# The first tile's statistics and output ahead of the pooled transposes' copies, and the fifth tile's matmuls beside the other output tiles

## The chip, the cores and the metric

One core of one Trainium2 chip runs the whole program. The metric is the device time of one execution in microseconds (us). Several executions of the changed kernel and of the kernel before are taken in turn on the same chip, and a separate profiled execution gives the trace. The engines are named as the profile names them: PE is TensorE's matmuls, PEld its weight loads, DVE is VectorE, ACT is ScalarE, POOL is GpSimd, SP issues DMAs. A line of a timeline gives start and length in us, engine, line of kernel.py, operation, tile written<-tiles read, shapes and count, and in brackets the engine's idle time before it with what ended it.

## The reference, cut to what matters

A linear attention with 32 memory slots feeds a two-layer network with a layer norm, over 8 batches of 576 rows and 512 columns.

```python
k_m = einsum('bhsm,bhsd->bhmd', a, k); v_m = einsum('bhsm,bhsd->bhmd', a, v)  # pooling, a = softmax(phi)
attn = softmax(scale * q @ k_m^T)                                             # scores
x = (attn @ v_m), heads side by side                                          # 8 x 576 x 512
xn = (x - mean(x)) / sqrt(var(x) + 1e-6) * g_ln
out = x + relu(xn @ w_ch1) @ w_ch2                                            # 512 -> 2048 -> 512
```

The kernel folds v_m and g_ln into w_ch1, so the first layer is computed from the attention weights, and it applies 1/sqrt(var) only at the end. That is why the statistics of x can come late: only the output needs them.

## The kernel before

A loop step handles batch b's layers and, between their matmuls, prepares batch b+1. The second layer (mm2) of a tile of 128 rows is 16 matmuls into `ch_ps`, cut into two halves of eight. The output of a tile adds x and frees its `ch_ps` buffer.

```python
def big(...): psum.tile(..., tag="big", bufs=3)    # kv_ps, o_ps, kvT_ps, sc_ps, w1b_ps, den_ps, h_ps
def one(...): psum.tile(..., tag="one", bufs=2)    # ch_ps

def x_tiles(pr, ts, stats=True):   # o_ps matmuls, then ACT copies o_ps to x_sb           (L420, L426)
def x_stats(pr, t):                # DVE: mean and variance of one tile                  (L439, L440)
def x_rstd(pr, ts):                # ACT: rstd = exp(-0.5 ln(var + eps)), two instructions (L445, L446)
def mm2_out(pr, t):                # DVE: x = ch_ps * rstd + x, then two output DMAs     (L483)
def a_kv(b):                       # PE pooling into kv_ps; DVE copies k, v, reciprocal  (L222, L227, L232)
def a_tr(b):                       # PE transposes k, v; DVE copies kvT, gain, row sums  (L261, L263, L267)
def a_sc(b):                       # PE scores from kvT; ACT exponentials E_sb           (L308, L313)
# ... a_den (L339), a_w1b (L369, L373), a_vb, mm1 (h_ps, L390)

for b in range(1, B):
    odd = b % 2; t = [4, 5, 6, 7, 8] if odd else [0, 1, 2, 3]
    mm1(b, ...)                    # ... 64 matmuls
    half(0);  a_kv(nb);  x_tiles(pr, t[0:2], False);  x_tiles(pr, t[2:4], False);  load(nb + 1)
    half(1);  a_tr(nb);  x_stats(pr, t[0]);  x_stats(pr, t[1]);  a_qT(nb + 1, 0)
    half(2);  a_sc(nb);  x_rstd(pr, t[0:2]);  a_w1b(nb, 0);  mm2_out(pr, t[0])
    half(3);  a_den(nb, finish=False);  mm2_out(pr, t[1]);  x_stats(pr, t[2])   # ...
    half(4);  a_den2(nb)           # half(4) is the third tile: it needs the first tile's ch_ps buffer
    if odd: x_tiles(pr, t[4:5], False)      # the fifth tile; else a_w1b(nb, 1..3)
    # ... half(5) to half(9)
```

Conditions on the first and last steps are cut above. In what follows, step one is b = 1 and step seven, the last, is b = 7. Steps one, three, five and seven are odd and have five tiles.

The softmax here doesn't subtract the row's maximum and nothing guards it: scores larger than these inputs give would overflow.

## Time and profile before

| | before |
|---|---|
| time, median of 3 runs | 253.18 us |
| start-up, to the first mm1 of the loop | 54.7 us |
| steps one to six | 30.05, 25.74, 29.64, 25.74, 29.64, 25.73 us |
| step seven, to the matmuls of its last tile (L471) | 22.89 us |
| the rest | 7.3 us |

The parts are those of the profiled execution, whose span on the core is 251.4 us (its time is 253.22). The step lengths are the distances between successive groups of h_ps matmuls in the chain of waits, which follows the work that ended last back through what released it, and has this form (start, length, what):

```profile
110.47 7.96 PE h_ps L390 x64
...
140.11 7.96 PE h_ps L390 x64
...
165.85 7.96 PE h_ps L390 x64
```

Step three is 140.11 − 110.47 = 29.64 us, step four 25.74 us.

### The profile page before, as it was taken

To read this page: it belongs to the slowest core of one execution; us is meant where nothing else is said; L and a number is where in the kernel's file an instruction comes from. 1 tells how busy PE (TensorE), PEld (TensorE's weight loads), DVE (VectorE), ACT (ScalarE), POOL (GpSimd) and SP (SyncE) were. 2 spreads that over 40 slices of the span, in tenths; PEclk is the share of its full clock that TensorE was granted. 3 is DMA by queue.
4 is the path that set the end of the run, shared out by engine and by line. 5 is a ranking of instruction groups with operands and counts; after the bars stand their busy time and mean duration, and the time that the engine had idled before them with its cause. 6 is when DMAs were issued, how large, how long until landed. Compare 5 with 4: busy or idle time off the path is not lost.

```text
span 251.4 us, 5829 instructions
## 1 busy us (share of the span) xinstructions
PE 236.0 (94%) x2446; PEld 131.6 (52%) x2477; DVE 155.1 (62%) x300; ACT 130.1 (52%) x219; POOL 60.0 (24%) x99
## 2 busy tenths in 40 slices
PE   7878999899999999999999999999999999999993
PEld 2443555447534665367534674467444764476453
DVE  3236773595397655787479646885679537873641
ACT  3154662677364464837382646655581755465220
POOL 8643231027204502090206302270205010000000
PEclk9999999999999999999999999999999999999999
DMA  7999999999996798739973998539892300303133
GB/s 148 192 206 207 206 257 215 282 212 128 211 193 128 130 256 182 146 53 202 249 147 89 142 252 136 123 43 223 200 188 44 78 8 0 86 16 71 44 81 83
DMA packets 41922, 36.82 MB, mean 146 GB/s; under 512 B 17444, under 2 KB 37160, under 8 KB 41896
## 3 DMA queue, kind: packets, MB, share of 16 engines
q0 software_dynamic: 17248, 19.53, 45.8%
q1 hardware_dynamic: 24488, 16.79, 29.2%
q8 instruction: 19, 0.31, 0.5%
q10 hardware_dynamic: 160, 0.13, 0.2%
q14 instruction: 7, 0.06, 0.1%
HBM read 41.42 MB, written 9.44 MB: 202 GB/s over the span
## 4 chain that ended last, share of the span: by engine, by line
PE 72%; DMA 17%; ACT 5%; DVE 2%; issue 2%; POOL 1%; POOLq 0%
PE ch_ps L459 41%; PE h_ps L390 22%; DMA q_bf<-in_q_dram 7%; DMA w2b<-in_moe_w_ch_dram 6%; ACT E_sb L313 4%; DMA kv_bf<-in_k_dram 3%; PE w1b_ps L369 2%; PE o_ps L420 2%; DVE x_sb L483 2%; PE kv_ps L205 2%; PE last_ps L471 1%; PE sc_ps L308 1%; POOL q_bf L92 1%; ACT rstd L446 1%; ACT rstd L445 0%
## 5 line engine op out<-in xcount | busy, mean ns | idle before, releaser
L459 PE MATMUL ch_ps<-w2b,rT 128*128 128x512 bf16 x531 | 123.4, 379 | 3.9 <-issue 1.7
L459 PEld LDWEIGHTS <-rT 128*128 128x128 bf16 x560 | 52.2, 98 | 64.5 <-issue 7.8
L390 PE MATMUL h_ps<-Eh,w1b 128*128 128x288 bf16 x512 | 66.7, 285 | 0.7 <-ACT rT L396 0.5
L396 ACT ACTIVATE rT<-h_ps 128x576 bf16<-128x576 f32 x88 | 52.5, 648 | 27.4 <-PE h_ps L390 27.3
L390 PEld LDWEIGHTS <-w1b 128*128 128x128 bf16 x512 | 49.6, 97 | 17.2 <-issue 2.0
L373 DVE SCALAR_TENSOR_TENSOR w1b<-m_sb,rsum,w1b_ps 128x512 bf16<-128x512 f32 x64 | 43.8, 743 | 6.4 <-PE w1b_ps L369 3.5
L398 DVE TENSOR_SCALAR rT<-h_ps 128x576 bf16<-128x576 f32 x40 | 30.3, 758 | 26.9 <-PE h_ps L390 26.3
L483 DVE SCALAR_TENSOR_TENSOR x_sb<-ch_ps,rstd,x_sb 128x512 f32<-128x512 f32 x35 | 25.6, 744 | 8.6 <-PE ch_ps L459 6.9
L426 ACT ACTIVATE x_sb<-o_ps 128x1024 f32<-128x1024 f32 (+1 forms) x20 | 17.8, 933 | 18.4 <-PE o_ps L420 18.4
L439 DVE BATCH_NORM_STATS2 bst<-x_sb 128x6 f32<-128x512 f32 x36 | 24.3, 676 | 3.1 <-ACT x_sb L426 3.1
L189 POOL TENSOR_TENSOR es<-e_sb 128x512 f32<-128x512 bf16 x6 | 6.9, 1156 | 68.1 <-ACT e_sb L182 68.1
L313 ACT ACTIVATE E_sb<-sc_ps,rs 128x640 bf16<-128x640 f32 x16 | 11.8, 790 | 19.5 <-PE sc_ps L308 19.5
L276 POOL TENSOR_TENSOR vb<-v,vmask 128x256 bf16<-128x256 bf16 x12 | 7.7, 662 | 57.3 <-DVE rs L232 57.3
L445 ACT ACTIVATE rstd<-mv,eps_sb 128x2 f32<-128x2 f32 (+1 forms) x20 | 5.9, 296 | 27.3 <-DVE mv L440 27.3
L355 DVE SCALAR_TENSOR_TENSOR Eh<-E_sb,rs,rden 128x576 bf16<-128x576 bf16 x16 | 12.4, 816 | 8.1 <-ACT rden L354 8.1
L174 PE MATMUL w_ps<-fill 128*128 128x512 f32 x14 | 9.8, 819 | 1.6 <-DVE fill L119 1.6
L369 PE MATMUL w1b_ps<-w1r,kvT 64*32 64x512 bf16 x256 | 10.7, 381 | 0.0
L222 DVE CAST k<-kv_ps 128x256 bf16<-128x256 f32 x7 | 3.0, 424 | 12.5 <-PE kv_ps L205 12.5
L182 ACT ACTIVATE e_sb<-phi_st 128x1152 bf16<-128x1152 f32 x8 | 9.2, 1152 | 2.7 <-DMA phi_st<-in_phi_dram 2.7
L354 ACT ACTIVATE rden<-rden 128x576 f32<-128x576 f32 x16 | 10.0, 673 | 0.1
L261 DVE COPY kvT<-kvT_ps 128x256 bf16<-128x256 bf16 x8 | 2.3, 292 | 12.2 <-PE kvT_ps L259 11.8
L92 POOL DMA_DIRECT2D q_bf<-in_q_dram x10 | 7.6, 761 | 4.6 <-DMA w2b<-in_moe_w_ch_dram 1.9
(73 smaller groups left out, 155.1 us busy)
## 6 DMA issues: line engine op xcount, KB each, us to landing
out_dram<-x_sb SPq DMA_DIRECT2D x70, 128.0 KB, 3.5
kv_bf<-in_k_dram POOLq DMA_DIRECT2D x7, 576.0 KB, 8.8
kv_bf<-in_v_dram POOLq DMA_DIRECT2D x7, 576.0 KB, 12.5
phi_st<-in_phi_dram SPq DMA_DIRECT2D x6, 576.0 KB, 10.5
q_bf<-in_q_dram POOLq DMA_DIRECT2D x6, 576.0 KB, 14.9
w1r<-in_moe_w_ch_dram POOLq DMA_DIRECT2D x4, 512.0 KB, 14.2
w2b<-in_moe_w_ch_dram POOLq DMA_DIRECT2D x4, 512.0 KB, 18.8
q_bf<-in_q_dram POOLq DMA_DIRECT2D x4, 288.0 KB, 12.7
```

What stands on the lines that cost most here:

```text
L92: nc.gpsimd.dma_start(out=t.rearrange("p j n x -> p j (n x)")[:, js, 0:NS * D], in_=rows(q, b)[:, js, :])
L313: nc.scalar.activation(out=E_[:, g].rearrange("p (a x) -> p a x", a=2), in_=sc[:, :, 0:HP], func=AF.Exp, scale=s["rs"][:, g:g + 1])
L355: nc.vector.scalar_tensor_tensor(out=Eh[:, g, :], in0=s["E"][:, g, 0:S], scalar=s["rs"][:, g:g + 1], in1=rd[:, g].rearrange("p a x -> p (a ...
L369: nc.tensor.matmul(ps[32 * j:32 * (j + 1), g, :], s["kvT"][r:r + 64, 2, 32 * j:32 * (j + 1)], w1r[r:r + 64, j, fs], start=True, stop=True, ...
L373: nc.vector.scalar_tensor_tensor(out=s["w1b"][:, g, fs], in0=m_sb[:, fs], scalar=s["rsum"][:, g:g + 1], in1=ps[:, g, :], op0=ALU.mult, op1 ...
L390: nc.tensor.matmul(h_ps[:, half, 0:HS], s["w1b"][:, g, P * j:P * (j + 1)], s["Eh"][:, g, HS * half:HS * (half + 1)], start=(g == 0), stop= ...
L396: nc.scalar.activation(out=dst, in_=h_ps[:, :, 0:HS], func=AF.Relu)
L398: nc.vector.tensor_scalar(out=dst, in0=h_ps[:, :, 0:HS], scalar1=0.0, scalar2=None, op0=ALU.max)
L426: nc.scalar.activation(out=x[:, 0:n].rearrange("p i (u y) -> p i u y", u=2), in_=o_ps.rearrange("p u (i y) -> p i u y", i=2)[:, 0:n], func ...
L439: nc.vector.bn_stats(out=stt, in_=x)
L459: nc.tensor.matmul(ch_ps, rT[:, j, P * t:P * (t + 1)], w2b[:, j, :], start=(j == 0), stop=(j == JC - 1))
L483: nc.vector.scalar_tensor_tensor(out=x, in0=ch_ps, scalar=rstd, in1=x, op0=ALU.mult, op1=ALU.add)
```

## The change

Its intent is to free the first `ch_ps` buffer earlier. The statistics of the first two tiles, their rstd and the first tile's output move ahead of work for the next batch, and in the odd steps the fifth tile's small group of o_ps matmuls joins the other two.

```diff
         x_tiles(pr, t[2:4], False)
+        if odd:
+            x_tiles(pr, t[4:5], False)
         ... loads ...
         half(1)
+        x_stats(pr, t[0])
+        x_stats(pr, t[1])
+        x_rstd(pr, t[0:2])
         if more:
             a_tr(nb)
-        x_stats(pr, t[0])
-        x_stats(pr, t[1])
         if nb + 1 < B:
             a_qT(nb + 1, 0)
+        mm2_out(pr, t[0])
         half(2)
         if more:
             a_sc(nb)
-        x_rstd(pr, t[0:2])
-        if more:
             a_w1b(nb, 0)
-        mm2_out(pr, t[0])
         half(3)
         ...
-        if odd:
-            x_tiles(pr, t[4:5], False)
-        else:
+        if not odd:
             a_w1b(nb, 1)
```

## The prediction

> **What bounds the kernel now.** I read the page first (busy times, slices, chain), then the chain of waits, then the timelines of TensorE, weight loads, VectorE and ScalarE over one step, and last the compiled instruction order of both kernels, which names each instruction's waits.
>
> The page says which engine to look at. In each line: engine, busy us, share of the span, instructions.
>
> ```profile
> PE 236.0 (94%) x2446; PEld 131.6 (52%) x2477; DVE 155.1 (62%) x300; ACT 130.1 (52%) x219; POOL 60.0 (24%) x99
> ...
> PEclk9999999999999999999999999999999999999999
> ```
>
> TensorE is busy for 94% at the full granted clock; no other engine exceeds 62%. After the start-up (mm1 of the loop's first step begins at 54.68 us) six steps alternate between about 25.7 and 29.6 us and a seventh ends the program. So a gap on TensorE in a steady step is paid six times. What the chain lists in the step that begins at 110.5 us, in order of time (start, us, what):
>
> ```profile
> 125.66 1.48 ACT E_sb L313 x2
> 127.13 0.19 ACT rstd L445
> 127.33 0.02 issue
> 127.35 0.21 ACT rstd L446
> 127.56 0.02 issue
> 127.59 0.76 DVE x_sb L483
> 128.35 0.04 issue
> 128.39 1.89 PE ch_ps L459 x8
> ```
>
> In this otherwise pure TensorE chain, a path through ScalarE and VectorE ends last once: the output of the first tile (L483), behind its rstd (L445, L446), behind the exponentials. The accumulator ch_ps has two buffers; the third tile's first matmul needs the buffer that the first tile's output frees. The TensorE and weight-load timelines size the stall:
>
> ```profile
> 127.70 0.44 PE L339 MATMUL den_ps<-E_sb,blk 64*64 64x288 bf16 x8
> 128.39 1.89 PE L459 MATMUL ch_ps<-w2b,rT 128*128 128x512 bf16 x8 [0.25 <-DVE x_sb L483]
> ```
>
> ```profile
> 128.07 0.10 PEld L459 LDWEIGHTS <-rT 128*128 128x128 bf16 x1 [0.23 <-issue]
> 128.39 1.39 PEld L459 LDWEIGHTS <-rT 128*128 128x128 bf16 x7 [0.23 <-issue]
> ```
>
> The weights of the first ch_ps matmul went in at 128.07, but it started at 128.39. At the un-stalled change from w1b_ps to ch_ps in this step, both fall within 0.01 us (125.86, 125.87). I therefore take 0.32 us, not the printed 0.25, which counts from the modelled end of den_ps. The waits list this gap six times, 1.5 us in all.
>
> VectorE in the same stretch shows why rstd is late, and that it need not be:
>
> ```profile
> 121.50 0.16 DVE L232 RECIPROCAL rs<-kv_ps 128x2 f32<-128x2 f32 x1
> 123.64 0.29 DVE L261 COPY kvT<-kvT_ps 128x256 bf16<-128x256 bf16 x1 [1.97 <-PE kvT_ps L259]
> 123.84 0.28 DVE L263 TENSOR_TENSOR kvT<-kvT_ps,g_bf 128x128 bf16<-128x128 bf16 x1
> 124.04 0.28 DVE L267 TENSOR_REDUCE rsum<-v 128x2 f32<-128x128 bf16 x1
> 124.23 0.68 DVE L439 BATCH_NORM_STATS2 bst<-x_sb 128x6 f32<-128x512 f32 x1
> ```
>
> VectorE sat idle 1.97 us before the kvT copy, while x_sb, which the statistics read, was ready from about 122.45.
>
> **What the Trainium skill says.** "TensorE: Matmul & The Clock Gate", section "Architectural detail: the array is 16× 32×32, not 1× 128×128": TensorE can pull weight loads ahead of running matmuls, and ScalarE and VectorE are strict first-in, first-out queues. The trace agrees: the weights at 128.07 went ahead of the stalled matmul, and the ready statistics stayed behind a copy waiting for TensorE. "Perfetto Trace Analysis", section "Identifying the Most-Contended Engine": the same gap repeating on the engine that should be saturated can mean too few buffers for the next tile. That fits a 0.25 us gap in six of six steps. "TensorEngine Tiling (Array Packing)", section "Key Properties": a change of tiling mode drains TensorE. The trace shows weight loads 0.42 us apart at the changes to L308, L339 and L420, so moving a small group between full-array groups is not free either way.
>
> **The change, part by part.** No instruction is added or removed; the compiled order only moves them.
>
> (a) Statistics of the first two tiles now precede the kvT copies. They wait for the first x_sb copy (ScalarE, from 121.42). In the last step of the kernel before, where no kvT copy stands between, statistics start 1.05 us after that copy starts (232.46 against 231.41) and two tiles' worth ends 1.71 later (234.17). So: start 122.47, end 124.18. The kvT copy, ready at 123.64, goes to about 124.09 and ends near 124.38, the gain product near 124.57. Scores load their weights at 125.25: slack 0.87 us, so a 0.45 us delay costs TensorE nothing.
>
> (b) rstd goes ahead of the exponentials on ScalarE: 124.22 to 124.74 (0.52, as in the last step). The exponentials start at 125.66 as before: slack 0.9.
>
> (c) The first output then starts near 124.78, after the row sums, and ends near 125.53 instead of 128.35. The third tile wants the buffer at 128.07, so the stall goes with 2.5 us to spare: 6 × 0.32 = 1.92 us. The last step has no such gap (output done 235.52, third tile from 236.50) and gains nothing here.
>
> (d) The fifth tile's o_ps group (four steps) moves forward to join the other o_ps matmuls. Removed: ch_ps would have continued at 128.39 + 8 × 0.2167 = 130.12 (spacing from x16 in 3.63 us with a 0.379 us last one), but resumed at 130.42, so 0.30. Added: four more matmuls at (0.76 − 0.62)/4 = 0.035, the groups of 20 and 16, so 0.14. But three "big" buffers rotate, and in the three odd steps with pooling the new tile gets kv_ps's buffer, free only after the reciprocal ends at 121.66. ch_ps loaded weights at 121.53; with 0.04 of signalling (as 128.35 to 128.39) the group starts at 121.70: a new stall of 0.17. Added 0.31, removed 0.30: zero in steps one, three and five. The last step has no kv_ps: 0.14 − 0.30 = −0.16.
>
> Sum: −1.92 − 0.16 = −2.1 us; 253.18 − 2.1 = 251.1.
>
> **The rivals.** First, TensorE waits at the scores instead, because kvT comes late. For it: the copies do move, and every score waits on them. If statistics had to wait for both x_sb copies (the second ends at 123.36), they would start 0.9 later, eating exactly the slack: up to 0.1 to 0.3 us a step, time 251.5 to 253. Against: the last step's statistics began with the first copy done and the second still running. I give it 10%.
>
> Second, the new kv_ps wait is larger than I sized it, since k, v and reciprocal all stand before it and weights must load after it. At 0.5 us a step it takes back 1 us: 252.1. The compiled order shows this wait on the weight load itself. 15%.
>
> Third, another limit stands just behind the stall and takes the gain. Candidates: den_ps against the exponentials (done 127.14, needed 127.63, slack 0.5, unmoved); in even steps the last w1b_ps reusing a den_ps buffer freed at 159.67 in the step from 140 us, wanted at 159.40 + 2 × 0.26 = 159.92 after the shift, slack 0.25. Both hold, the second barely. The time would be 252 to 253. 10%.
>
> Fourth, output transfers start about 2 us earlier where the queue is free and collide with loads. The loads feed a later step and no DMA is in the chain after 47 us, so I expect nothing.
>
> **Range and chances.** The gain cannot much exceed 6 × 0.32 plus the removed groups, 4 × 0.30, so about 3 us (250.1) if the new wait were nil and the added matmuls free; 2% would need 5.1 us. To be slower by 2% every step would need a new 0.8 us stall on top, which no slack above suggests. Allowing part of rivals one to three upward and 0.5 downward: 250.6 to 252.4, predicted 251.2, rounding toward the rivals. Faster 0.01, same 0.98, slower 0.01.
>
> **What would show it.** Right: the six ch_ps waits on x_sb L483 vanish; weights and first matmul of the third tile start together; statistics fill VectorE's idle before the kvT copy, which falls from 1.97 us to nearly none; kvT ends 0.4 to 0.5 later with no new wait at L308; an o_ps wait on the reciprocal appears three times at about 0.17; odd steps shorten by about 0.32, even steps by 0.32, the last by 0.16. Wrong: a TensorE wait on kvT at L308, an o_ps wait of 0.4 or more, a w1b_ps wait on den_ps, or even steps that shorten by less than 0.25.

## The result, and the profile after

The changed kernel takes 251.25 us (median of 4 runs, 250.98 to 251.51) against 253.23 us for the kernel before in the same rounds. The ratio is 0.9919, with a 95% interval of 0.9900 to 0.9938. A ratio is the mean time of one kernel's runs over the mean of the other's in the same rounds, so it isn't quite the ratio of the medians quoted. By the 2% measure that is "same"; the gain of 0.8% is nevertheless clear of noise.

The busy line of the changed kernel's page says that TensorE is still the bound, at 94% of the span as before. The busy total itself, down from 236.0 us, is no measure of the gain: in the seven steps it fell by only 0.67 us (184.80 to 184.13), the rest of the difference is in the start-up, and the repeat of the changed kernel printed 236.3.

```profile
PE 234.5 (94%) x2446; PEld 131.5 (53%) x2477; DVE 155.1 (62%) x300; ACT 130.7 (52%) x219; POOL 60.0 (24%) x99
```

Where the time went is seen in the steps. From the chain of waits of the changed kernel, the same three groups:

```profile
109.98 7.96 PE h_ps L390 x64
...
139.40 7.96 PE h_ps L390 x64
...
164.83 7.96 PE h_ps L390 x64
```

Step three is 29.42 us (0.22 less), step four 25.43 (0.31 less). All seven, in us:

| kernel | 1 | 2 | 3 | 4 | 5 | 6 | 7 | sum |
|---|---|---|---|---|---|---|---|---|
| before | 30.05 | 25.74 | 29.64 | 25.74 | 29.64 | 25.73 | 22.89 | 189.43 |
| changed | 29.83 | 25.43 | 29.42 | 25.43 | 29.43 | 25.42 | 22.68 | 187.64 |

The steps together are 1.79 us shorter. Next, the place of the stall. The weight loads of the changed kernel in step three (start, length, what, and in brackets the idle time before with what ended it):

```profile
127.62 0.14 PEld L339 LDWEIGHTS <-blk 64*64 64x64 bf16 x8 [0.42 <-issue]
127.99 4.86 PEld L459 LDWEIGHTS <-rT 128*128 128x128 bf16 x24 [0.22 <-issue]
```

Before, one load of the third tile stood alone at 128.07 and the other seven came from 128.39. Now its weights run on in one piece with those of the groups after it (x24), the list of waits has no ch_ps wait on L483 any more, and the chain no longer leaves TensorE in this step:

```profile
127.62 0.44 PE den_ps L339 x8
128.06 5.29 PE ch_ps L459 x24
```

VectorE of the changed kernel in the same step shows how the buffer came free:

```profile
121.02 0.16 DVE L232 RECIPROCAL rs<-kv_ps 128x2 f32<-128x2 f32 x1
121.98 0.69 DVE L439 BATCH_NORM_STATS2 bst<-x_sb 128x6 f32<-128x512 f32 x1 [0.81 <-ACT x_sb L426]
...
123.60 0.26 DVE L261 COPY kvT<-kvT_ps 128x256 bf16<-128x256 bf16 x1
...
124.29 0.75 DVE L483 SCALAR_TENSOR_TENSOR x_sb<-ch_ps,rstd,x_sb 128x512 f32<-128x512 f32 x1
```

The statistics fill most of the idle time that stood before the kvT copy; 0.81 us of it is left, ahead of them, until x_sb is there. The copy then follows without a wait, and the output is done at 125.04, 2.95 us before the third tile wants the buffer at 127.99.

What was paid for it stands at the o_ps group. The weight loads of step three before, then after:

```profile
120.84 0.58 PEld L420 LDWEIGHTS <-Eh 64*64 64x64 bf16 x20
121.53 1.41 PEld L459 LDWEIGHTS <-rT 128*128 128x128 bf16 x8
```

```profile
120.35 0.58 PEld L420 LDWEIGHTS <-Eh 64*64 64x64 bf16 x20
121.23 0.11 PEld L420 LDWEIGHTS <-Eh 64*128 64x128 bf16 x4 [0.30 <-DVE rs L232]
121.45 1.41 PEld L459 LDWEIGHTS <-rT 128*128 128x128 bf16 x8
```

From the first o_ps weights to those of ch_ps it was 0.69 us and is now 1.10: the fifth tile's group costs 0.41 here. It waits for the reciprocal that empties kv_ps, because with three rotating buffers it was given that one.

### The profile page after: what moved, and what is told of

The parts are those of the page before. It is cut to its first block, busy times and chain, and to the rows that moved or that the text cites. A ratio compares the mean times of both kernels' runs of the same rounds, so it can differ in the third digit from the quotient of the medians.

```text
span 249.7 us, 5829 instructions
## 1 busy us (share of the span) xinstructions
PE 234.5 (94%) x2446; PEld 131.5 (53%) x2477; DVE 155.1 (62%) x300; ACT 130.7 (52%) x219; POOL 60.0 (24%) x99
## 4 chain that ended last, share of the span: by engine, by line
PE 77%; DMA 17%; issue 2%; DVE 1%; POOL 1%; ACT 0%; POOLq 0%
PE ch_ps L459 44%; PE h_ps L390 22%; DMA q_bf<-in_q_dram 7%; DMA w2b<-in_moe_w_ch_dram 6%; DMA kv_bf<-in_k_dram 4%; PE w1b_ps L369 3%; PE kv_ps L205 2%; PE last_ps L471 1%; PE o_ps L420 1%; PE sc_ps L308 1%; PE den_ps L339 1%; POOL q_bf L92 1%; DVE k L222 1%; PE den_ps L326 0%; PE qT_ps L293 0%
## 5 line engine op out<-in xcount | busy, mean ns | idle before, releaser
L373 DVE SCALAR_TENSOR_TENSOR w1b<-m_sb,rsum,w1b_ps 128x512 bf16<-128x512 f32 x64 | 43.8, 743 | 8.4 <-PE w1b_ps L369 6.2
L483 DVE SCALAR_TENSOR_TENSOR x_sb<-ch_ps,rstd,x_sb 128x512 f32<-128x512 f32 x35 | 26.1, 746 | 9.9 <-PE ch_ps L459 6.7
L174 PE MATMUL w_ps<-fill 128*128 128x512 f32 x14 | 9.0, 755 | 1.6 <-DVE fill L119 1.6
L205 PE MATMUL kv_ps<-kv_bf,e_sb 64*32 64x128 bf16 (+1 forms) x648 | 7.4, 215 | 0.6 <-DMA kv_bf<-in_v_dram 0.3
```

The source lines that it names most:

```text
L205: nc.tensor.matmul(ps[32 * j:32 * (j + 1), g, 0:D * (sl.stop - sl.start)], e[r:r + TS, c, j, :], kv[r:r + TS, j, sl, D * c:D * (c + 1)], s ...
L373: nc.vector.scalar_tensor_tensor(out=s["w1b"][:, g, fs], in0=m_sb[:, fs], scalar=s["rsum"][:, g:g + 1], in1=ps[:, g, :], op0=ALU.mult, op1 ...
L483: nc.vector.scalar_tensor_tensor(out=x, in0=ch_ps, scalar=rstd, in1=x, op0=ALU.mult, op1=ALU.add)
```

## The experiments

The theory under test: the gain is six removed stalls of about 0.31 us on a `ch_ps` buffer; removing them takes both the early statistics and the early rstd and output; and the fifth tile's group, moved along, gives 0.09 us back in three steps and wins 0.21 in the last. The rivals: the group carries the gain; one half of the reordering suffices; kvT, which now comes later, is on the edge; the group costs the same wherever it stands. Ten runs were made, the last of them the changed kernel once more, each for five timed rounds, in three sets (chips 4, 4 and 6), each with the kernel before beside it. All gave correct results.

| run | time, median us | before beside it | ratio (95%) | odd (3), even (4), last step |
|---|---|---|---|---|
| group put back | 251.28 | 253.26 | 0.9923 (0.9901 to 0.9945) | 29.34, 25.43, 22.89 |
| group alone | 253.15 | 253.26 | 0.9988 (0.9964 to 1.0012) | 29.73, 25.73, 22.67 |
| statistics alone | 253.22 | 253.26 | 0.9991 (0.9968 to 1.0013) | 29.64, 25.74, 22.88 |
| rstd and output alone | 252.50 | 253.26 | 0.9959 (0.9934 to 0.9984) | 29.55, 25.64, 22.88 |
| group before the pooling | 251.32 | 253.10 | 0.9939 (0.9921 to 0.9958) | 29.34, 25.43, 22.78 |
| group early in last step only | 250.96 | 253.10 | 0.9931 (0.9909 to 0.9952) | 29.34, 25.43, 22.67 |
| three tiles' statistics first | 251.62 | 253.10 | 0.9947 (0.9930 to 0.9963) | 29.42, 25.43, 22.67 |
| four tiles' statistics first | 254.62 | 253.10 | 1.0057 (1.0041 to 1.0072) | 29.75, 26.17, 22.66 |
| k and v emptied in one copy | 250.90 | 253.14 | 0.9903 (0.9872 to 0.9933) | 29.29, 25.43, 22.67 |
| changed kernel again | 251.62 | 253.14 | 0.9931 (0.9900 to 0.9962) | 29.42, 25.43, 22.67 |

Read the last column first. The changed kernel itself came out at 251.25 and at 251.62 us in two sets, so times cannot tell a few tenths apart. The step lengths can.

### The group put back in its old place

Against the changed kernel:

```diff
-        if odd:
-            x_tiles(pr, t[4:5], False)      # beside the other x_tiles
...
-        if not odd:
+        if odd:
+            x_tiles(pr, t[4:5], False)      # after half(4)
+        else:
```

> The changed kernel with the fifth tile's o_ps group put back to its old place. Theory (the gain is the six ch_ps stalls of 0.32 us; the moved group gives back about 0.10 in steps one, three and five through its wait on kv_ps, and wins 0.21 in the last step): odd and even steps both shorten by 0.32 against the kernel before (even 25.43, odd 29.32 us), the last step stays at 22.89, and the time is within 0.2 us of the changed kernel, about 251.2. Rival (the earlier eviction of the fifth tile is what lets the steps run closer): odd steps return to about 29.6 and the time rises to 252 or more.

Measured: even steps 25.43, odd 29.34, last 22.89, and 251.28 us. The reordering of statistics, rstd and output alone takes 0.30 to 0.32 us off each steady step, which is the size of the stall, and keeps the whole time gain. The rival that the early eviction of the fifth tile matters falls.

### The group moved alone

The kernel before with only the two `x_tiles` parts of the change: the fifth tile's group is taken out after half(4) and put beside the other `x_tiles`.

> The kernel before with only the fifth tile's group moved. Theory: the six ch_ps stalls on x_sb stay; an o_ps wait on the reciprocal appears in steps one, three and five; odd steps lengthen by 0.1 (29.74), even steps stay at 25.74, the last step shortens by 0.21 (22.68); time 253.2 to 253.4. Rival (the group carries the gain): odd steps near 29.3, time near 252.

Measured: odd 29.73, even 25.73, last 22.67, each within 0.01 us of what was expected; the time, 253.15 us, is 0.05 below the range given. Both waits stand side by side in the list of waits of TensorE and of its weight loads (who waited for whom: us in total, times, longest):

```profile
PE ch_ps L459 <- DVE x_sb L483: 1.5, 6, 0.3
...
PEld L420 <- DVE rs L232: 0.9, 3, 0.3
```

The two parts add up: the steps of the first run are 1.84 us shorter than before (187.59 against 189.43), those of this run 0.03 longer (189.46), together 1.81; the changed kernel has 1.79.

### The statistics moved alone

Against the kernel before:

```diff
+        x_stats(pr, t[0])
+        x_stats(pr, t[1])
         if more:
             a_tr(nb)
-        x_stats(pr, t[0])
-        x_stats(pr, t[1])
```

> The kernel before with only the statistics of the first two tiles moved ahead of the kvT copies; rstd and output stay behind the exponentials. Theory (the stall's path runs through the exponentials on ScalarE, not through VectorE's copies): the ch_ps wait on x_sb stays in all six steps, even steps 25.74, time 253.2. Rival (late statistics are the cause by themselves): even steps 25.43 and about 251.4.

Measured: every step as before within 0.01 us, 253.22 us, and the `ch_ps` wait on L483 is listed as before with 1.5 us in six times. Statistics that end 1.75 us sooner in step three (13.71 us after it begins, not 15.46) are worth nothing while rstd stands behind the exponentials in ScalarE's queue.

### rstd and output moved alone

Against the kernel before:

```diff
         x_stats(pr, t[1])
+        x_rstd(pr, t[0:2])
         if nb + 1 < B:
             a_qT(nb + 1, 0)
+        mm2_out(pr, t[0])
         half(2)
         ...
-        x_rstd(pr, t[0:2])
         ...
-        mm2_out(pr, t[0])
```

> The kernel before with only rstd and the first output moved ahead of the scores; the statistics stay behind the kvT copies. Theory (both halves are needed: statistics end 125.93 in the step from 110.5, so rstd holds the exponentials until 126.49 instead of 125.66, they end near 127.97, and den_ps, wanted at 127.70, waits about 0.3): the ch_ps wait on x_sb goes, a den_ps wait on E_sb of about 0.3 comes in its place, steps within 0.1 of before, time 253.0 to 253.4. Rival (moving the output alone carries the gain): no den_ps wait, even steps 25.43, time about 251.4.

Measured: 252.50 us, and each steady step 0.10 us shorter. The time is below the range that I gave, so this expectation was partly missed. The wait on x_sb goes and one on the exponentials takes its place, as the theory has it, but it is smaller. ScalarE and then the weight loads of this run in step three:

```profile
126.43 1.46 ACT L313 ACTIVATE E_sb<-sc_ps,rs 128x640 bf16<-128x640 f32 x2
```

```profile
127.73 0.35 PEld L339 LDWEIGHTS <-blk 64*64 64x64 bf16 x8 [0.42 <-issue]
128.31 1.41 PEld L459 LDWEIGHTS <-rT 128*128 128x128 bf16 x8 [0.23 <-issue]
```

The den_ps weights are spread over 0.35 us, where they took 0.14 before, and from their start to those of ch_ps it is 0.58 us against the un-stalled 0.37 (127.70 to 128.07). So den_ps waits 0.21, not my 0.3: the exponentials end at 127.89, not 127.97. (The list of waits does not name this wait; it lies inside the den_ps group.) A stall of 0.31 has become one of 0.21. Both halves of the reordering are needed for the whole gain; the second alone brings a third of it.

This run moved rstd and the output together, and no run moved them apart. In the kernel before, the two w1b copies (L373) that stood ahead of the output end at 127.42. An output directly behind them would end near 128.2 by the 0.76 us that it took there, about 0.15 late for the 128.07 at which the third tile loads its weights. This is an estimate: what the output's own move is worth is not shown.

### The group ahead of the pooling

Against the changed kernel:

```diff
         half(0)
+        if odd:
+            x_tiles(pr, t[4:5], False)
         if more:
             a_kv(nb)
         x_tiles(pr, t[0:2], False)
         x_tiles(pr, t[2:4], False)
-        if odd:
-            x_tiles(pr, t[4:5], False)
```

> The changed kernel with the fifth tile's o_ps group moved once more, to stand ahead of the pooling matmuls, so that it takes a buffer that is long free and the last o_ps group waits only for an eviction begun early. Theory (the 0.09 us that the moved group costs an odd step is its wait on kv_ps's buffer): the o_ps wait on the reciprocal goes; odd steps fall from 29.42 to about 29.28 (29.34 with the group in its old place, less 0.30 for the group removed there, plus 0.14 for four matmuls[...]); even steps stay at 25.43, the last at 22.68; time 250.8 to 251.2. Rival (the extra cost is the additional group itself, wherever it stands): odd steps stay at 29.42 or more.

Measured: odd 29.34, even 25.43, last 22.78, 251.32 us. The weight loads of step three in this run:

```profile
120.00 0.12 PEld L420 LDWEIGHTS <-Eh 64*128 64x128 bf16 x4 [0.42 <-issue]
120.22 0.11 PEld L242 LDWEIGHTS <-hl 128*128 128x128 bf16 x2
```

The wait on the reciprocal is gone and the odd step is 0.08 shorter than in the changed kernel, so the wait did cost. But the step is not below the 29.34 of the group in its old place; my 29.28 was 0.06 too hopeful, and the time is 0.12 above the range given. (The terms in the expectation give 29.18; the other 0.1 was an allowance.) Standing apart from the other o_ps matmuls, the group costs what it cost at its old place, and the last step loses 0.10 of what it had won. Here the expectation and its rival are each half right, so the wait needed an experiment that leaves the group where it is (below).

### The group early in the last step only

Against the version with the group put back: the fifth tile's `x_tiles` stands beside the others `if last`, and after half(4) `if odd and more`.

> Statistics, rstd and output early in all steps, the fifth tile's group early in the last step alone, where no kv_ps stands in its way. Theory: odd steps 29.34, even 25.43, last 22.68, so 0.2 us below the version with the group in its old place and 0.25 below the changed kernel: about 251.0. Rival (the last step's gain comes from something other than the group): last step 22.89.

Measured: odd 29.34, even 25.43, last 22.67, 250.96 us. The last step gains 0.22 by the group alone, where no kv_ps is in the rotation.

### Three and four tiles' statistics ahead of the copies

Against the changed kernel:

```diff
         x_rstd(pr, t[0:2])
+        x_stats(pr, t[2])                 # first dose
+        x_stats(pr, t[3])                 # second dose, in the second of the two runs
         if more:
             a_tr(nb)
```

with the later `x_stats` of these tiles taken out.

> A dose of rival one: the changed kernel with the third tile's statistics ahead of the kvT copies too, which delays those by another 0.8 us. In the changed kernel the kvT copy ends at 123.86 and the scores load weights at 125.17, slack 1.3. Theory (slack is real): the copy ends near 124.67, no new wait at the scores, steps unchanged (even 25.43, odd 29.42), time about 251.2. Rival (kvT is already on the edge): each step lengthens by several tenths, time 253 or more.

> The double dose: the third and the fourth tile's statistics ahead of the kvT copies, 1.6 us in all, more than the slack of 1.3. Theory: the kvT copy ends near 125.48, the scores' weights wait on it from 125.17 to about 125.52, and each of the six steps lengthens by 0.3 to 0.45 us (even 25.75 to 25.9, odd 29.75 to 29.9); the last step stays at 22.68; time 253.0 to 253.9. Rival (kvT never reaches TensorE's path): steps as in the changed kernel, 251.2.

Measured: the first dose leaves the steps as in the changed kernel (29.42, 25.43, 22.67); its time, 251.62 us, is 0.4 above what was expected, and the same as that of the changed kernel's repeat. The second gives odd steps 29.75, as expected, but even steps 26.17, beyond the 25.75 to 25.9 that I gave, and 254.62 us, also beyond my range: a miss in size. The waits of that run:

```profile
PEld L308 <- DVE kvT L261: 6.3, 7, 1.2
```

The miss has a plain cause, which the changed kernel's own trace shows. I took the slack, 1.3 us, from an odd step. Its even step four reads (VectorE, then weight loads):

```profile
152.90 0.26 DVE L261 COPY kvT<-kvT_ps 128x256 bf16<-128x256 bf16 x1
```

```profile
154.06 0.14 PEld L308 LDWEIGHTS <-kvT 64*32 64x32 bf16 x16 [0.42 <-issue]
```

The copy ends at 153.16 and is wanted at 154.06, so an even step has a slack of 0.90. In an odd step the fifth tile's group holds TensorE 0.41 longer between the x_sb tiles that the statistics read and the scores, which matches the other 0.4. Two tiles' statistics are 1.60 us in step four of this run (155.72 − 154.12 between starts). With about 0.04 of signalling, 1.60 − 0.90 + 0.04 is 0.74 and 1.60 − 1.31 + 0.04 is 0.33: the measured lengthening of even (26.17 − 25.43) and of odd steps (29.75 − 29.42). So the first rival names a real path; the change stays 0.9 us clear of it.

### k and v emptied in one copy

Against the changed kernel, for the batches of the steady steps:

```diff
-        k_out(b, ps, b < 2)                # copies k twice, side by side
-        v_out(b, ps[:, :, D:2 * D])
-        rs_out(b, ps)
+        kvs = att.tile([P, 2, 2, D], BF16, name="kvs")
+        nc.vector.tensor_copy(out=kvs.rearrange("p s g d -> p g s d"), in_=<k and v of ps>)
+        rs_out(b, ps)                      # kv_ps is free here
+        nc.vector.tensor_copy(out=k2, in_=<k of kvs, twice>)
```

> The changed kernel, with kv_ps emptied by one VectorE copy of k and v together and the reciprocal; the doubling of k is done afterwards from the copy. kv_ps's buffer then comes free about 0.2 us sooner (0.34 + 0.16 after the copy starts instead of 0.69), near where the fifth tile's group wants it. Theory (that group's cost in odd steps is the wait on kv_ps): the o_ps weights' gap falls from 0.30 by 0.15 to 0.2, odd steps fall from 29.42 to 29.2 to 29.3, below the 29.34 with the group in its old place; even steps, which have no such wait, stay at 25.43 within 0.02 (the control), the last at 22.68; about 0.5 us below the changed kernel run beside it. Rival (the cost is the group itself): odd steps stay at 29.42.

Measured: odd 29.29, even 25.43, last 22.67, all as expected; 250.90 us, 0.72 below the changed kernel beside it where 0.5 was expected. Step one, not in the table, fell by 0.19 (29.83 to 29.64). VectorE and weight loads of step three in this run (the lines after its edit are numbered nine higher, so L420 is L429 here):

```profile
120.23 0.42 DVE L251 CAST kvs<-kv_ps 128x256 bf16<-128x256 f32 x1 [1.81 <-PE kv_ps L205]
120.58 0.16 DVE L232 RECIPROCAL rs<-kv_ps 128x2 f32<-128x2 f32 x1
```

```profile
120.04 0.58 PEld L429 LDWEIGHTS <-Eh 64*64 64x64 bf16 x20
120.79 0.11 PEld L429 LDWEIGHTS <-Eh 64*128 64x128 bf16 x4 [0.17 <-DVE rs L232]
```

The reciprocal now starts 0.35 us after the copy, against 0.54 before (120.48 to 121.02), and the gap ahead of the fifth tile's weights falls from 0.30 to 0.17, a little less than the 0.15 to 0.2 expected. The odd step falls by the same 0.13, with the group at the same place, and the even step, the control, does not move. The wait on kv_ps is thereby shown to be what made the moved group cost more in odd steps than it saved. This version has the lowest time of all (250.90) and the shortest steps (187.17 us in sum); it is below both kernels, though only the steps, not the overlapping intervals of the times, separate it from the changed kernel.

### The changed kernel again

> The changed kernel again, beside the version above and the kernel before on the same chip: steps 29.42, 25.43 and 22.68, ratio 0.992 within 0.002; shows how far a difference of a few tenths can be trusted in the times.

Measured: the steps repeat to 0.01 us, the ratio is 0.9931, inside what was expected, and the median 251.62.

## Why the prediction was right

The predicted 251.2 us stands against 251.25 and, in the repeat, 251.62 measured; both lie in its range. That the first of them is only 0.05 us away is partly luck: the terms added up to 2.1 us and the steps gave 1.79, but the number had been rounded up by 0.1, and the start-up moves by tenths. By its own steps:

- **(a) Statistics ahead of the kvT copies.** Right. It put the kvT copy 0.45 us later with 0.87 of slack left. In even step four the copy starts 1.04 us after the transposes' first weights (151.86 to 152.90), where before it was 0.58 (152.57 to 153.15): 0.46 later, slack 0.90. In step three it starts 0.45 later after the step's beginning (13.17 to 13.62) but hardly later after the transposes' first weights (0.59 to 0.63), since the moved group delays these and the scores too. The double dose shows the slack to be real and of this size.
- **(b) and (c) rstd and output early, six stalls gone.** Right: 6 × 0.32 was expected, and the version without the group's move gained 1.84 in the steps. The printed idle time of 0.25 would have given 1.5. Reading the stall from the weight load that had gone ahead was the better choice. Neither the statistics alone (nothing) nor rstd and output alone (0.10 a step) would have done it. One reading of (b) was off without harm: in step three the exponentials start 0.41 later after the step's beginning than before (15.19 to 15.60), held back with the scores by the moved group.
- **(d) The fifth tile's group.** The mechanism was right, one size was off. Removing it at its old place was put at 0.30, its matmuls at the new place at 0.14 and the wait on kv_ps at 0.17, a balance of zero in an odd step. Measured by the weights in step three, the new place costs 0.41: a wait of 0.19 beyond where ch_ps would have begun (120.35 + 0.69 = 121.04, to 121.23) and 0.22, not 0.14, from there to the ch_ps weights. The term that was mis-sized is the four matmuls: I took their cost from groups that run on without a stop, but after a wait they cost what they cost standing alone (0.21 from 130.21 to 130.42 before). So odd steps shortened by 0.22 rather than by 0.32. In the last step, with no wait, the same stretch grew from 0.69 (230.83 to 231.52) to 0.79 us (229.30 to 230.09), so there they cost 0.10, and the gain was 0.21 against 0.16 expected. The list of waits prints 0.30 for the wait, because it counts from the end of the previous weights; 0.17 was reckoned from where ch_ps would have begun.
- **The rivals.** The first and the third did not come true: no new wait at the scores, none of den_ps on the exponentials, none of w1b_ps on den_ps. (For the third, den_ps was said to be needed at 127.63; its weights stand at 127.70, so the slack was 0.56 and not 0.5.) The second hardly did: the wait itself was 0.19 and not 0.17, and the change gave back 0.09 in each of three steps. As to the fourth, the first output's transfers were issued 2.4 us earlier in step four (15.36 us after it begins, not 17.77), while in step three, behind the transposing load of qT, they came 0.6 later; in both kinds of step the lengths are accounted for without them.
- **The page on repeating gaps.** The prediction takes from "Perfetto Trace Analysis" that such a gap can mean too few buffers for the next tile; the passage stands in its section "Optimization Strategy". The gap did concern a pair of buffers, but no buffer was added: emptying one of the two sooner closed all six.

The sum of the predicted terms was 2.1 us; the steps gave 1.79. The medians of the two sets gave 1.98 and 1.52, which the start-up, different by tenths from run to run, is enough to blur.

## What to carry to other kernels

When the saturated engine waits once per step, follow the wait back through every queue it passes and ask which instruction stood in front in each: here one wait needed a move in VectorE's and in ScalarE's order together, and one move alone brought nothing or a third. Before moving a group of matmuls, count the rotating buffers to see whose buffer it will get, and how soon that one is emptied. Judge tenths of a microsecond by distances between the same instructions in successive steps, not by the time of the run.

## What the Trainium skill lacked or had wrong

- "TensorEngine Tiling (Array Packing)", section "Key Properties", says that a change of tiling mode drains TensorE, but gives no cost. Here a group of four matmuls in the 64x128 mode between full-array groups cost 0.30 us, the matmuls included; appended to other o_ps matmuls it cost about 0.1 (moving it shortened the last step by 0.21), and behind a wait 0.22.
- "Perfetto Trace Analysis", section "Tensor Engine Instruction (MATMUL, LD_WEIGHTS)", says that the end of a matmul is an estimate. It doesn't say what follows for gaps: the printed idle time was 0.25 us where removing the stall brought 0.31. The weight load that had gone ahead gave 0.32.
